# The third product of a fused attention and two-MLP kernel by Strassen's seven products instead of eight

## The chip, the cores and the metric

One Trainium2 chip, one of its cores. The metric is the device time of one execution in microseconds (us). TensorE (PE) multiplies, VectorE (DVE) and ScalarE (ACT) do the elementwise work, GpSimd (POOL) helps, SyncE (SP) issues all DMAs from one instruction queue.

## The reference

Attention with a sliding window of 128 and a linear bias, then two MLPs in sequence, all in float32, for 2304 tokens (4 batches of 576):

```python
x = attention(q, k, v)                     # (2304, 512), 8 heads of 64
y = ((x @ w1) * (x @ w2)) @ w3 @ w_out     # 512 -> 1024 -> 1024 -> 512
h = y @ w_in                               # 512 -> 2048
out = (h * clip(h + 3, 0, 6) / 6) @ w_out2 # 2048 -> 512
```

## The kernel before

The engines run the order in which a scheduler has put the program's instructions; each engine's queue is in order, and waits are on semaphores.

**Number format.** Every float32 operand of the MLPs is kept as two float32r parts, `hi` and `lo`: `split` (L73) makes `hi` by an ACT copy and `lo` by a DVE subtraction. `mm3` (L45) forms a product by three matmuls (lines L46, L47, L48): hi*hi, then hi*lo and lo*hi in one order or the other. The weights arrive as 64-bit words; `unpack` (L54) turns 128x1024 of them into float32 with one ACT pass (L63) and two DVE passes (L64 shift, L68 shift and OR), in place in a tile named `raw...`.

**First stage** (to about 500 us). Attention per pair of heads, `w3 @ w_out` multiplied out into `Wh`, `Wl`, then per batch and per half `s` of its tokens (288): eight `ab_unit`s, which give g = (x w1)(x w2), and four `y_unit`s (L420), one per 128 columns of y. A `y_unit` is 24 matmuls of 288 columns into a PSUM bank; ACT copies the sum out and a DMA stores it to the DRAM tensor `yT`, laid out [channel group, 128, token].

**Second stage** (from about 500 us). Tokens go in five blocks `j` (four of 512, one of 256), the 2048 columns of h in 16 groups `f` of 128. `h_unit(j, f)` (L523) is 12 matmuls of the block's width (4 channel groups, three matmuls each); then ACT makes relu(h + 3) (`rl`, L536), DVE takes min(.., 6) * h (L537), and `split` gives the two parts of g2. `o_unit(j, f)` (L543) runs two units later: for each 128 tokens, three matmuls of 512 columns into one of four PSUM banks that stay open over all 16 `f`. Two further pairs of banks (`ps_mm`, `ps_h`) serve h in turn. All 16 groups' weights stay in SBUF (`v2`); `p2_make` unpacks and splits them, nine items during the last batch, the others beside block 0. `y_load` and `y_split` bring each block of y back from DRAM.

The order is that of this loop:

```python
for idx, (j, f) in enumerate(units):
    h_unit(j, f)
    if idx >= LAG:
        o_unit(*units[idx - LAG])
    if j == 0:
        p2_make(f + len(AT), vpool)
```

Of the kernel before, what the change touches and what calls it, by code (L numbers as in the profile page):

```python
# [22 lines left out]
def tile_attention_moe_moe2(ctx: ExitStack, tc: tile.TileContext, qT, kT, vm, vt, wo, w3, w12, w2x, out):  # L23
# [412 lines left out]
    def v2_load(f, tmp):
        load(("v2", f), w2x[f], tmp)

    def v2_split(f, pool, lo_eng):
# [6 lines left out]
        split(flat(hi), flat(lo), unpack(rawt.pop(("v2", f)), pinned=True), lo_eng)
        v2[f] = (hi, lo)

    blocks = [(t, min(TB, NT - t)) for t in range(0, NT, TB)]
    yb = {}  # L450

    yraw = {}

    p2 = [("v", f) for f in range(KG)]
    p2.insert(NPRE, ("y", 0))

    def p2_load(i):
        if i < len(p2):
            (v2_load if p2[i][0] == "v" else y_load)(p2[i][1], dec)

    def p2_make(i, pool):
        if i < len(p2):
            if p2[i][0] == "v":
                v2_split(p2[i][1], pool, nc.vector)
            else:
                y_split(0, pool)
            p2_load(i + 2)

    def y_load(j, tmp):
        t0, n = blocks[j]  # L470
        t = tmp.tile([P, KD, TB], F32, tag="raw", name=f"yraw{j}")
        nc.sync.dma_start(out=t[:, :, 0:n], in_=yT[:, :, t0 : t0 + n].rearrange("c p t -> p c t"))
        yraw[j] = t

    def y_split(j, pool):
        t0, n = blocks[j]
        yh = pool.tile([P, KD, TB], F32R, tag="yh2", bufs=1, name=f"yh2_{j}")
        yl = pool.tile([P, KD, TB], F32R, tag="yl2", bufs=1, name=f"yl2_{j}")
        t = yraw.pop(j)
        for i in range(2):  # L480
            c = slice(2 * i, 2 * i + 2)
            nc.scalar.copy(yh[:, c, 0:n], t[:, c, 0:n])  # L482
# [154 lines left out]
```

## Time and profile before

| | us |
|---|---|
| median of 3 runs (lowest, highest) | 895.56 (895.0, 897.57) |
| the profiled execution: its time | 896.03 |
| its span, from the first to the last instruction | 894.2 |
| PE busy, share of the span | 874.9 (98%) |
| DVE, ACT, POOL busy | 356.1, 357.2, 128.1 |
| DMA: moved, mean rate | 66.9 MB, 75 GB/s |
| mean granted clock of TensorE | 0.998 of 2.4 GHz |

The profiled execution is 0.47 us above the median, and 1.83 us of its time lie outside its span. PE is busy in nearly all of the span; busy time of a matmul includes the drain that its successor overlaps, so the time that a matmul takes of PE is the distance from one start to the next, not its duration.

### The profile page before, as it was taken

What the parts mean: (1) busy time and instruction counts of PE and PEld (TensorE: products, weight loads), DVE (VectorE), ACT (ScalarE), POOL (GpSimd) and SP (SyncE); (2) the same over time, 40 slices, a digit from 0 to 9 for tenths busy, and PEclk for the clock granted to TensorE, in tenths of its full rate; (3) what the DMA queues carried; (4) which work ended last, traced back from release to release, by engine and by line L of the source; (5) the groups of instructions that cost most, each with busy time, mean ns of one, the idle gap of its engine ahead of it and who ended that gap; (6) DMA issues with size and microseconds to landing.
All of it is one profiled execution on the core that took longest, in us unless ns stands there. A gap on an engine that the chain in (4) does not pass through costs nothing.

```text
span 894.2 us, 13104 instructions
## 1 busy us (share of the span) xinstructions
PE 874.9 (98%) x5216; PEld 734.8 (82%) x5216; DVE 356.1 (40%) x821; ACT 357.2 (40%) x784; POOL 128.1 (14%) x198
## 2 busy tenths in 40 slices
PE   6799999999999999999999999999999999999998
PEld 3344598889888898999999888888888888888897
DVE  4896543342433424121536585232223222322232
ACT  6764654453444434321344565322232222222232
POOL 4361132321321312100020002200020001000000
PEclk9999999999999999999999999999999999999999
DMA  6975201211211110003244465020001000100000
GB/s 252 358 289 207 88 26 54 80 41 40 67 57 50 42 41 2 27 1 122 72 144 143 138 218 188 1 71 1 1 1 47 1 1 1 47 1 1 24 25 24
DMA packets 23277, 66.91 MB, mean 75 GB/s; under 512 B 2480, under 2 KB 8112, under 8 KB 18608
## 3 DMA queue, kind: packets, MB, share of 16 engines
q1 hardware_dynamic: 23216, 66.07, 21.2%
q8 instruction: 41, 0.67, 0.3%
q14 instruction: 20, 0.16, 0.1%
HBM read 56.62 MB, written 9.44 MB: 74 GB/s over the span
## 4 chain that ended last, share of the span: by engine, by line
PE 95%; DMA 2%; DVE 1%; ACT 1%; POOL 0%; issue 0%; SPq 0%; ACTq 0%; DVEq 0%; POOLq 0%
PE ab L46 8%; PE ab L47 8%; PE ab L48 8%; PE o L46 7%; PE o L48 7%; PE o L47 7%; PE h L46 7%; PE h L48 7%; PE h L47 7%; PE wps L321 6%; PE s L133 4%; PE y L46 4%; PE y L48 4%; PE y L47 4%; PE X L223 3%; PE pt L200 3%
## 5 line engine op out<-in xcount | busy, mean ns | idle before, releaser
L46 PE MATMUL ab<-xh,w12h 128*128 128x288 f32 x512 | 156.1, 305 | 0.0
L48 PE MATMUL ab<-xh,w12l 128*128 128x288 f32 x512 | 151.4, 296 | 0.0
L47 PE MATMUL ab<-xl,w12h 128*128 128x288 f32 x512 | 151.3, 296 | 0.0
L536 ACT ACTIVATE rl<-h,three 128x512 f32<-128x512 f32 (+1 forms) x80 | 51.7, 647 | 200.1 <-PE h L48 196.2
L537 DVE SCALAR_TENSOR_TENSOR rl<-rl,h 128x512 f32<-128x512 f32 (+1 forms) x80 | 50.6, 634 | 200.3 <-ACT rl L536 200.3
L46 PE MATMUL h<-yh,v2h 128*128 128x512 f32 (+1 forms) x320 | 118.5, 370 | 0.5 <-DVE rl L537 0.5
L48 PE MATMUL h<-yh,v2l 128*128 128x512 f32 (+1 forms) x320 | 118.2, 369 | 0.0
L47 PE MATMUL h<-yl,v2h 128*128 128x512 f32 (+1 forms) x320 | 117.9, 369 | 0.0
L46 PE MATMUL o<-v2h,g2h 128*128 128x512 f32 x288 | 112.9, 392 | 0.0
L47 PE MATMUL o<-v2l,g2h 128*128 128x512 f32 x288 | 112.3, 390 | 0.0
L48 PE MATMUL o<-v2h,g2l 128*128 128x512 f32 x288 | 111.6, 391 | 0.0
L46 PEld LDWEIGHTS ab<-xh,w12h 128*128 128x128 f32 x512 | 96.4, 188 | 9.4 <-issue 5.5
L47 PEld LDWEIGHTS ab<-xl,w12h 128*128 128x128 f32 x512 | 96.6, 189 | 0.5 <-issue 0.2
L48 PEld LDWEIGHTS ab<-xh,w12l 128*128 128x128 f32 x512 | 96.5, 188 | 0.0
L183 POOL TENSOR_SCALAR pr<-pr,rc 128x256 f32<-128x256 f32 (+1 forms) x128 | 70.0, 565 | 173.6 <-DVE rc L176 137.4
L46 PE MATMUL y<-g,Wh 128*128 128x288 f32 x256 | 76.0, 300 | 0.2 <-ACT yf L427 0.2
L47 PE MATMUL y<-g,Wh 128*128 128x288 f32 x256 | 75.1, 295 | 0.0
L48 PE MATMUL y<-g,Wl 128*128 128x288 f32 x256 | 75.0, 294 | 0.0
L75 DVE TENSOR_TENSOR g2l<-rl,g2h 128x512 fp32r<-128x512 f32 (+1 forms) x80 | 54.8, 685 | 44.8 <-ACT g2h L74 44.5
L416 DVE TENSOR_TENSOR asb<-ab,asb 128x288 f32<-128x288 f32 x64 | 29.3, 457 | 106.8 <-PE ab L48 104.7
L167 ACT ACTIVATE pr<-pr,mn 128x256 f32<-128x256 f32 (+1 forms) x128 | 60.4, 475 | 26.8 <-DVE mn L158 26.8
L483 POOL TENSOR_TENSOR yl<-yraw,yh 128x1024 fp32r<-128x1024 f32 (+1 forms) x10 | 24.1, 2428 | 326.7 <-ACT yh L482 326.7
(73 smaller groups left out, 1332.9 us busy)
## 6 DMA issues: line engine op xcount, KB each, us to landing
raww<-in_w_dram SPq DMA_DIRECT2D x16, 1024.0 KB, 6.2
rawv<-in_w2x_dram SPq DMA_DIRECT2D x16, 1024.0 KB, 4.9
qw<-in_qT_dram SPq DMA_DIRECT2D x16, 288.0 KB, 2.8
kw<-in_kT_dram SPq DMA_DIRECT2D x16, 288.0 KB, 3.2
yT<-yf SPq DMA_DIRECT2D x32, 144.0 KB, 1.8
out_dram<-ob SPq DMA_DIRECT2D x18, 256.0 KB, 2.0
vw<-in_vm_dram SPq DMA_DIRECT2D x16, 256.0 KB, 2.6
rawwo<-in_wo_dram SPq DMA_DIRECT2D x4, 1024.0 KB, 8.6
```

The lines of the kernel that those rows point to most:

```text
L46: nc.tensor.matmul(ps, lh, rh, start=first, stop=False)
L47: nc.tensor.matmul(ps, lh, rl, start=False, stop=False)
L48: nc.tensor.matmul(ps, ll, rh, start=False, stop=last)
L75: lo_eng.tensor_tensor(out=lo, in0=src, in1=f32(hi), op=ALU.subtract)
L133: in_order(n == NP + 1 and js[0] == 0 or not head, nc.tensor.matmul(ps[:, h, i, 0:nk], qw[n % 2][HB[h], P * j : P * (j + 1)], kw[n % 2][HB ...
L167: nc.scalar.activation(o, o, AF.Exp, bias=mn[:, col : col + 1], scale=-1.0, accum_out=sm[:, col : col + 1])
L183: nc.gpsimd.tensor_scalar(out=o, in0=o, scalar1=rc[:, 2 * j + h : 2 * j + h + 1], scalar2=1.0, op0=ALU.mult, op1=ALU.mult)
L200: nc.tensor.transpose(ps[:, o : o + P], prob[n, j][:, h, c : c + P], ident)
L321: nc.tensor.matmul(ps[:, 0:DM], w3v[i][:, m, :], wov[m], start=m == 0, stop=m == KF - 1)
L416: nc.vector.tensor_tensor(out=asb, in0=pss[1][:, 0:HS], in1=asb, op=ALU.mult)
L536: nc.scalar.activation(rl[:, 0:n], ps[:, 0:n], AF.Relu, bias=three[:, 0:1], scale=1.0)
L537: nc.vector.scalar_tensor_tensor(out=rl[:, 0:n], in0=rl[:, 0:n], scalar=6.0, in1=ps[:, 0:n], op0=ALU.min, op1=ALU.mult)
```

## The change

h is formed by Strassen's scheme in Winograd's form. The two halves of the columns of `w_in` (group p and group p + 8), the two halves of the 512 channels and the two halves of the tokens make a 2x2x2 product; seven products of half size take the place of eight. The halves of the tokens are the halves `s` of each batch, so that the sums of y that the scheme needs are formed where both halves are at hand, in `y_unit`, by eight DVE operations per batch (two for the columns d < 2, six for the others); seven tensors are stored (`yT`, now [2, 7, 128, 1152]). The sums of the weights are formed when a pair's words are unpacked (`va_make`: four DVE operations of 256 columns), kept as seven tiles in hi and lo, and stored to DRAM (`vad`; the output weights of the pair go to `vod`), because they don't fit in SBUF; each of the three token blocks reads them back pair by pair (`fetch`), but block 0 reads back only pairs 1 and 2. The blocks are 384 columns of both halves, so 768 tokens.

A unit is now a pair p in a block j: `h_pair` runs the seven products, each of 6 matmuls of 384 columns, in two PSUM banks (unit 0 also borrows two others), and between them as many of the previous unit's twelve output jobs as `QUOTA` says (a job: three matmuls of 512 columns, for 128 tokens and one half of the pair). Five DVE operations per unit (`u2`, `u3`, `c22`, `c21`, `c12`) add the products up, four gates follow as before but 384 wide. Six PSUM banks hold the outputs. In the last batch three pairs are made beforehand (`EARLY`), and `ab_unit` and `y_unit` use four PSUM banks there instead of two.

```diff
+    def bank(b, name):
+        nbank[0] += 1
+        if b < B - 1 or nbank[0] % 4 < 2:
+            return ps_mm.tile([P, 512], F32, tag="mm", name=name)
+        return ps_o.tile([P, 512], F32, tag=f"o{nbank[0] % 4}", name=name)
...
     def y_unit(b, s, d):
...
-        yf = sp.tile([P, HS], F32, tag="yf", name=f"yf_{b}_{s}_{d}")
-        nc.scalar.copy(yf, ps[:, 0:HS])
-        t0 = b * S + s * HS
-        nc.sync.dma_start(out=yT[d, :, t0 : t0 + HS], in_=yf)
...
+        if s == 0:
+            ys[d] = new(f"y0{d}")
+            nc.scalar.copy(ys[d], ps[:, 0:HS])
+            put(ys[d], Y11 if d < 2 else Y21)
+        elif d < 2:
+            ys["t", ci] = new(f"t1{ci}")
+            nc.vector.tensor_tensor(out=ys["t", ci], in0=ps[:, 0:HS], in1=ys[ci], op=ALU.subtract)
+            put(ys["t", ci], YT1)
+        else:
+            y22, t2, t3, t4 = (new(t) for t in ("y22", "t2", "t3", "t4"))
+            nc.scalar.copy(y22, ps[:, 0:HS])
+            put(y22, Y22)
+            nc.vector.tensor_tensor(out=t2, in0=y22, in1=ys["t", ci], op=ALU.subtract)
+            put(t2, YT2)
...
+    PRODUCTS = [(A11, Y11), (S2, YT2), (A12, Y21), (S3, YT3), (S1, YT1), (A22, YT4), (S4, Y22)]
+    EARLY = [1, 2, 0]
+    FIRST = [0, 1, 3, 4, 2, 5, 6, 7]
...
+    def va_make(p, n):
+        r = unpack(rawt.pop(("v2", 2 * p)), pinned=True)
+        t = va_tile(n)
+        c = [slice(i * 2 * P, (i + 1) * 2 * P) for i in range(4)]
+        sub = lambda o, a, b, op=ALU.subtract: nc.vector.tensor_tensor(out=r[:, c[o]], in0=r[:, c[a]], in1=r[:, c[b]], op=op)
+        split(flat(t[:, 0, 0:2, :]), flat(t[:, 1, 0:2, :]), r[:, 0 : 4 * P], nc.vector)
+        split(t[:, 0, A22, :], t[:, 1, A22, :], r[:, c[3]], nc.vector)
+        sub(3, 2, 3, ALU.add)
+        sub(2, 0, 2)
+        sub(0, 3, 0)
+        sub(1, 1, 0)
+        split(flat(t[:, 0, 3:7, :]), flat(t[:, 1, 3:7, :]), r, nc.vector)
+        late.append((vad[p], t))
+
+    def vo_make(p, n):
+        r = unpack(rawt.pop(("v2", 2 * p + 1)), pinned=True)
+        t = vo_tile(n)
+        split(flat(t[:, 0, :, :]), flat(t[:, 1, :, :]), r, nc.vector)
+        late.append((vod[p], t))
...
+    def h_pair(j, p, n, between):
...
+                mm3(
+                    ps[:, 0:TH], w[:, 0, k, cols], w[:, 1, k, cols], yh[:, c, :], yl[:, c, :],
+                    first and c == 0, last and c == 1, skip_group_check=True,
+                )
...
+        a, b_ = bank(0), None
+        product(0, a, True, True)
+        s1 = new("s1")
+        nc.scalar.copy(s1, a[:, 0:TH])
+        between(0)
+        b_ = bank(1)
+        product(1, b_, True, True)
+        u2 = new("u2")
+        nc.vector.tensor_tensor(out=u2, in0=b_[:, 0:TH], in1=s1, op=ALU.add)
+        between(1)
+        product(2, a, False, True)
+        gate(a[:, 0:TH], (0, 0))
+        between(2)
+        product(3, b_, False, True)
+        u3 = new("u3")
+        nc.vector.tensor_tensor(out=u3, in0=b_[:, 0:TH], in1=s1, op=ALU.add)
+        between(3)
+        a = bank(2)
+        product(4, a, True, True)
+        c = new("c22")
+        nc.vector.tensor_tensor(out=c, in0=a[:, 0:TH], in1=u3, op=ALU.add)
+        gate(c, (1, 1))
...
+    QUOTA = [2, 2, 2, 1, 2, 2, 1]
...
+    MAKE = {0: ("a",), 1: ("o", "a"), 2: ("o",), 3: ("a",), 4: ("o", "a"), 5: ("o", "a"), 6: ("o",)}
...
+    for n, (j, p) in enumerate(units2):
+        fetch(n + 2, "a")
+        if n > 0:
+            fetch(n + 1, "o")
...
+            if n % NPR == NPR - 1 and j + 1 < NBLK:
+                y_split(j + 1, k)
...
+        gs = h_pair(j, p, n, between)
+        jobs = o_jobs(j, n, gs)
```

`MAKE` says beside which unit the words of the five pairs left are made; `y_split` makes one of the next block's seven tiles after each product of a block's last unit.

Three places show what moves. **SyncE, at the end of the last `y_unit`** (`rawv`: words of weights; `yT`: stores of y; `va`, `vo`: a unit's tiles). Before:

```order
L429 DMA yT_63<-yf_3_1_1_5059 128x288
L429 DMA yT_63<-yf_3_1_2_5096 128x288
L289 DMA rawv2_9_5069<-in_w2x_dram 128x1024
L429 DMA yT_63<-yf_3_1_3_5124 128x288
L289 DMA rawv2_10_5167<-in_w2x_dram 128x1024
```

Now:

```order
L447 DMA yT_63<-t4_3_1_2_5193 128x288
L710 DMA vo1_5257<-vod_65 128x2048
L447 DMA yT_63<-y22_3_1_3_5227 128x288
L485 DMA vad_64<-va0_4762 128x3584
L447 DMA yT_63<-t2_3_1_3_5228 128x288
L447 DMA yT_63<-t3_3_1_3_5229 128x288
L447 DMA yT_63<-t4_3_1_3_5230 128x288
```

The last four stores of y stand behind a load of 1.05 MB, which waits for the last y matmul, and three of them behind a store of 1.84 MB as well.

**VectorE, at the start of the second stage** (`rl`: the gate's min and multiply; `c22`, `c21`, `u2`, `u3`: sums of products). Before:

```order
L537 SCALAR_TENSOR_TENSOR rl_0_0_5153<-rl_0_0_5153,h_0_0_5140 128x512
L537 SCALAR_TENSOR_TENSOR rl_0_1_5182<-rl_0_1_5182,h_0_1_5169 128x512
L75 TENSOR_TENSOR g2l_0_0_5155<-rl_0_0_5153,g2h_0_0_5154 128x512
L64 TENSOR_SCALAR rawv2_8_5004<-rawv2_8_5004 128x1024
L68 SCALAR_TENSOR_TENSOR rawv2_8_5004<-rawv2_8_5004 128x1024
```

Now:

```order
L635 TENSOR_TENSOR u2_0_0_5276<-h_0_0_1_5269,s1_0_0_5266 128x384
L64 TENSOR_SCALAR rawv2_6_4773<-rawv2_6_4773 128x1024
L68 SCALAR_TENSOR_TENSOR rawv2_6_4773<-rawv2_6_4773 128x1024
L618 SCALAR_TENSOR_TENSOR rl_0_0_5301<-rl_0_0_5301,h_0_0_0_5259 128x384
L642 TENSOR_TENSOR u3_0_0_5314<-h_0_0_1_5269,s1_0_0_5266 128x384
L75 TENSOR_TENSOR va2_5282<-rawv2_6_4773,va2_5282 128x512
L647 TENSOR_TENSOR c22_0_0_5323<-h_0_0_2_5316,u3_0_0_5314 128x384
L75 TENSOR_TENSOR va2_5282<-rawv2_6_4773,va2_5282 128x256
L653 TENSOR_TENSOR c21_0_0_5338<-u3_0_0_5314,h_0_0_3_5331 128x384
L505 TENSOR_TENSOR rawv2_6_4773<-rawv2_6_4773 128x256
```

The first gate stands behind two passes over the words of the third unit's weights, and the sums that follow stand between the making of those weights.

**VectorE, in one unit of block 1**, where no weights are made. Before, the same two rows for each `f`:

```order
L537 SCALAR_TENSOR_TENSOR rl_1_7_5961<-rl_1_7_5961,h_1_7_5948 128x512
L75 TENSOR_TENSOR g2l_1_7_5963<-rl_1_7_5961,g2h_1_7_5962 128x512
L537 SCALAR_TENSOR_TENSOR rl_1_8_5993<-rl_1_8_5993,h_1_8_5980 128x512
L75 TENSOR_TENSOR g2l_1_8_5995<-rl_1_8_5993,g2h_1_8_5994 128x512
L537 SCALAR_TENSOR_TENSOR rl_1_9_6025<-rl_1_9_6025,h_1_9_6012 128x512
```

Now:

```order
L635 TENSOR_TENSOR u2_1_3_6767<-h_1_3_1_6760,s1_1_3_6752 128x384
L618 SCALAR_TENSOR_TENSOR rl_1_3_6781<-rl_1_3_6781,h_1_3_0_6745 128x384
L75 TENSOR_TENSOR g2_1_3_00_6782<-rl_1_3_6781,g2_1_3_00_6782 128x384
L642 TENSOR_TENSOR u3_1_3_6799<-h_1_3_1_6760,s1_1_3_6752 128x384
L647 TENSOR_TENSOR c22_1_3_6811<-h_1_3_2_6804,u3_1_3_6799 128x384
L618 SCALAR_TENSOR_TENSOR rl_1_3_6813<-rl_1_3_6813,c22_1_3_6811 128x384
L75 TENSOR_TENSOR g2_1_3_11_6814<-rl_1_3_6813,g2_1_3_11_6814 128x384
L653 TENSOR_TENSOR c21_1_3_6832<-u3_1_3_6799,h_1_3_3_6825 128x384
L658 TENSOR_TENSOR c12_1_3_6852<-h_1_3_2_6804,u2_1_3_6767 128x384
```

The sum that frees the bank of the unit's last product, `c12`, has moved ahead of the gates of `c21` and of itself. On PE the unit's output jobs stand between the products much as `QUOTA` has them; the scheduler puts the two matmuls that need only g2's hi part of three jobs ahead of the three that need its lo part.

## Rows read from the trace of the kernel before

**Rows 1.** Windows, second stage: us, engines' busy time (instructions), PEclk, DMA share, GB/s

```profile
504.34:890.00 385.66, 385.66 (x1776) 319.83 (x1776) 132.47 (x191) 124.52 (x191) 18.32 (x8) 1.00 0.11 37
```

**Rows 2.** The same stretches, instructions on h alone

```profile
504.34:890.00 385.66, 201.76 (x912) 159.98 (x912) 49.88 (x79) 50.42 (x78) 1.00 0.11 37
```

**Rows 3.** PE in order of time, last batch: start, us, engine, line, operation

```profile
457.81 0.29 PE L48 MATMUL ab<-xh,w12l 128*128 128x288 f32 x1
...
458.87 0.30 PE L47 MATMUL ab<-xl,w12h 128*128 128x288 f32 x1
```

**Rows 4.** In order of time, block 1: matmuls of 512, one gate

```profile
642.10 0.39 PE L46 MATMUL h<-yh,v2h 128*128 128x512 f32 x1
...
644.60 0.39 PE L48 MATMUL h<-yh,v2l 128*128 128x512 f32 x1
...
645.09 0.69 ACT L536 ACTIVATE rl<-h,three 128x512 f32<-128x512 f32 x1 [3.37 <-PE h L48]
...
645.80 0.69 DVE L537 SCALAR_TENSOR_TENSOR rl<-rl,h 128x512 f32<-128x512 f32 x1 [3.37 <-ACT rl L536]
...
646.53 0.62 ACT L74 CAST g2h<-rl 128x512 fp32r<-128x512 f32 x1 [0.76 <-DVE rl L537]
...
647.18 0.69 DVE L75 TENSOR_TENSOR g2l<-rl,g2h 128x512 fp32r<-128x512 f32 x1 [0.69 <-ACT g2h L74]
```

**Rows 5.** Weight loads for h: duration min/median/max in ns

```profile
L46 PEld LDWEIGHTS h<-yh,v2h x320: 186/188/192, 454.2 to 885.3; 128*128 128x128 f32 x160
```

**Rows 6.** In order of time, start of the second stage

```profile
502.88 1.26 ACT L536 ACTIVATE rl<-h,three 128x512 f32<-128x512 f32 x2 [3.84 <-DMA yT<-yf]
...
503.50 0.39 PE L48 MATMUL h<-yh,v2l 128*128 128x512 f32 x1
503.60 1.29 DVE L537 SCALAR_TENSOR_TENSOR rl<-rl,h 128x512 f32<-128x512 f32 x2 [6.41 <-ACT rl L536]
...
504.34 0.50 PE L46 MATMUL h<-yh,v2h 128*128 128x512 f32 x1 [0.46 <-DVE rl L537]
```

**Rows 7.** DVE groups by shape: busy us, mean ns | idle before

```profile
L416 DVE TENSOR_TENSOR asb<-ab,asb 128x288 f32<-128x288 f32 x64 | 29.3, 457 | 106.8 <-PE ab L48 104.7 <-ACT pr L167 1.1 <-PE pt L200 0.8
...
L75 DVE TENSOR_TENSOR v2l<-rawv,v2h 128x1024 fp32r<-128x1024 f32 x16 | 20.0, 1249 | 11.6 <-ACT v2h L74 11.6
L68 DVE SCALAR_TENSOR_TENSOR rawv<-rawv 128x1024 int32<-128x1024 int32 x16 | 19.6, 1226 | 7.1 <-ACT rawv L63 6.4
...
L64 DVE TENSOR_SCALAR rawv<-rawv 128x1024 int32<-128x1024 int32 x16 | 11.1, 691 | 2.1 <-DMA rawv<-in_w2x_dram 2.0
...
L75 DVE TENSOR_TENSOR g2l<-rl,g2h 128x256 fp32r<-128x256 f32 x16 | 6.8, 425 | 7.1 <-ACT g2h L74 7.1
L537 DVE SCALAR_TENSOR_TENSOR rl<-rl,h 128x256 f32<-128x256 f32 x16 | 6.7, 421 | 23.7 <-ACT rl L536 23.7
```

**Rows 8.** ACT groups by shape

```profile
L536 ACT ACTIVATE rl<-h,three 128x256 f32<-128x256 f32 x16 | 7.6, 477 | 23.3 <-PE h L48 23.2
...
L74 ACT CAST g2h<-rl 128x256 fp32r<-128x256 f32 x16 | 6.5, 407 | 7.5 <-DVE rl L537 7.5
```

**Rows 9.** DMA issues: KB each, median us to landing

```profile
rawv<-in_w2x_dram SPq DMA_DIRECT2D x16, 1024.0 KB, 4.9
...
yT<-yf SPq DMA_DIRECT2D x32, 144.0 KB, 1.8
out_dram<-ob SPq DMA_DIRECT2D x18, 256.0 KB, 2.0
```

**Rows 10.** SyncE in order of time at the end of the last y

```profile
497.22 0.42 SPq L289 DMA_DIRECT2D rawv<-in_w2x_dram  x1
```

**Rows 11.** The chain that ended last, the same place

```profile
499.06 3.71 DMA yT<-yf
```

**Rows 12.** Windows at the start

```profile
34.60:38.00 3.40, 3.34 (x4) 1.49 (x5) 3.40 (x12) 2.99 (x9) 1.51 (x4) 0.52 1.00 402
```

**Rows 13.** PE in order of time at the start

```profile
34.66 5.83 PE L321 MATMUL wps<-wov,w3v 128*128 128x512 f32 x9 [2.23 <-DVE w3v L68]
```

More of the change, by code (lines that the diff above doesn't have):

```diff
@@ new lines, in tile_attention_moe_moe2, with dma @@
+    NBLK = 3
+    TH = NT // 2 // NBLK
+    NTT = TH // P
+    A11, A12, A22, S2, S4, S3, S1 = range(7)
+    PRODUCTS = [(A11, Y11), (S2, YT2), (A12, Y21), (S3, YT3), (S1, YT1), (A22, YT4), (S4, Y22)]
+    EARLY = [1, 2, 0]
+    FIRST = [0, 1, 3, 4, 2, 5, 6, 7]
+    ORDER = [FIRST, list(range(NPR)), list(range(NPR))]
+    units2 = [(j, p) for j in range(NBLK) for p in ORDER[j]]
+    place = {p: n for n, p in enumerate(FIRST)}
+    va = {}
+    vo = {}
+    p1_open = [True]
+    late = []
+    def dma(dst, src):
+        in_order(not p1_open[0], nc.sync.dma_start(out=dst, in_=src))
@@ L441, in v2_split, with y_split @@
+    def y_split(j, i):
         hi, lo = (
-            (blk if old else pool).tile(
-                [P, 2 * KD, P], F32R, name=f"v2{t[0]}{f}", **({"tag": f"{t}{f - NPRE}"} if old else {})
-            ) for t in ("hi", "lo")
-        )
[L446 to L482, printed above, removed]
-            nc.gpsimd.tensor_tensor(out=yl[:, c, 0:n], in0=t[:, c, 0:n], in1=f32(yh[:, c, 0:n]), op=ALU.subtract)
-        yb[j] = (yh, yl)
+            blk.tile([P, 2, TH], F32R, tag=f"{t}{i}", name=f"y{t}{j}_{PRODUCTS[i][1]}") for t in ("hi", "lo")
+        )
@@ L561, in tile_attention_moe_moe2 @@
[L561 to L575 removed]
+    g2p = ctx.enter_context(tc.tile_pool(name="g2p", bufs=8))
@@ new lines, in tile_attention_moe_moe2, with product, new, gate @@
+    po = {}
+    ob_ = {}
+    def h_pair(j, p, n, between):
+        w = va[n]
+        def product(i, ps, first, last):
+            k, y = PRODUCTS[i]
+            yh, yl = yc[j, y]
+            for c in range(2):
+                cols = slice(c * P, (c + 1) * P)
+                mm3(
+                    ps[:, 0:TH], w[:, 0, k, cols], w[:, 1, k, cols], yh[:, c, :], yl[:, c, :],
+                    first and c == 0, last and c == 1, skip_group_check=True,
+                )
+        def new(tag):
+            return r2.tile([P, TH], F32, tag=tag, bufs=2 if tag in ("rl", "u2", "u3") else 1, name=f"{tag}_{j}_{p}")
+        gs = {}
+        def gate(h, q):
+            rl = new("rl")
+            g_ = g2p.tile([P, 2, TH], F32R, tag="g2", name=f"g2_{j}_{p}_{q[0]}{q[1]}")
+            nc.scalar.activation(rl, h, AF.Relu, bias=three[:, 0:1], scale=1.0)
+            nc.vector.scalar_tensor_tensor(out=rl, in0=rl, scalar=6.0, in1=h, op0=ALU.min, op1=ALU.mult)
+            split(g_[:, 0, :], g_[:, 1, :], rl, nc.vector)
+            gs[q] = g_
+        def bank(i):
+            if n == 0 and i >= 2:
+                return ps_o.tile([P, 512], F32, tag=f"o{i + 2}", name=f"h_{j}_{p}_{i}")
+            return ps_mm.tile([P, 512], F32, tag="mm", name=f"h_{j}_{p}_{i}")
+        a, b_ = bank(0), None
[20 more added lines that the diff above has]
+        gate(c, (1, 1))
+        between(4)
+        b_ = bank(3)
+        product(5, b_, True, True)
+        c = new("c21")
+        nc.vector.tensor_tensor(out=c, in0=u3, in1=b_[:, 0:TH], op=ALU.subtract)
+        gate(c, (1, 0))
+        between(5)
+        product(6, a, False, True)
+        c = new("c12")
+        nc.vector.tensor_tensor(out=c, in0=a[:, 0:TH], in1=u2, op=ALU.add)
+        gate(c, (0, 1))
+        between(6)
+        return gs
@@ new lines, in tile_attention_moe_moe2, with fetch @@
+    QUOTA = [2, 2, 2, 1, 2, 2, 1]
+    def fetch(n, which):
+        if n >= len(units2) or n == 0:
+            return
+        j, p = units2[n]
+        if j == 0 and p not in EARLY:
+            return
+        t, src = (va_tile(n), vad) if which == "a" else (vo_tile(n), vod)
+        in_order(n > 1, nc.sync.dma_start(out=f32(t), in_=src[p]))
+    MAKE = {0: ("a",), 1: ("o", "a"), 2: ("o",), 3: ("a",), 4: ("o", "a"), 5: ("o", "a"), 6: ("o",)}
+    fetch(1, "a")
+    fetch(1, "o")
+    jobs = []
@@ L578 @@
+    for job in jobs:
+        job()
 _OUTS = [((2304, 512), "float32")]
```

197 lines of the change are left out of this document (121 added, 76 removed).

## The prediction

> **What bounds the kernel now.** I read first the windows of the second stage, then the order of time at its two ends, then the groups by shape. In the windows the reader is to see that PE's busy time is the window itself [rows 1]: 385.66 us, 1776 matmuls, no idle. VectorE is busy for a third of it and the DMA engines for 0.11. So the second stage costs what its matmuls cost in PE's row, and nothing else. Of these 1776, 912 are h's [rows 2] (720 of 512 columns, 192 of 256; 48 of block 0's ran earlier) and 864 are o's of 512 columns, together 860,160 columns. 385.66 us / 860,160 is 0.4484 ns a column, 0.2296 us for 512. The one wait between the stages is 0.46 us, for VectorE, which waited for ScalarE, which waited for the last store of y [rows 6].
>
> **What is removed.** h is now 768 matmuls of 512 columns and 192 of 256: 442,368 columns, at 0.4484 ns 198.3 us. After, 24 units of 7 products of 6 matmuls are 1008 matmuls of 384 columns, 387,072 columns, 7/8. No row has a width of 384. The nearest are 288 with 0.1325 us (eight distances in 458.87 - 457.81 [rows 3]) and 512 with 0.2296. A line between them gives 0.1741 us, so 175.5 us, **22.8 us less**. Bounds: the rate of the fastest stretch of 512 (eleven distances in 2.50 us [rows 4], 0.444 ns a column) gives 0.1705 us and 26.4 less; the rate of 288 (0.460 ns) gives 0.1766 and 20.2 less. I take the line, since 384 lies halfway. The outputs keep 864 matmuls of 512 columns, 198.4 us. A unit is then 42 x 0.1741 + 36 x 0.2296 = 15.58 us.
>
> The order of weight load and matmul could speak against this. A weight load lasts 188 ns [rows 5], more than a matmul of 384 would take; but matmuls of 288 follow each other every 132 ns, each with weights of its own, so the load does not set the pace there, and I keep the saving. The Trainium skill, "TensorE: Matmul & The Clock Gate", section "Back-to-back issue gap", says that in a stream of weight loads and matmuls both set the spacing; the row of 288 columns decides against that here, the rival below prices it. The same section gives for a matmul alone columns / 2.4 + 2.5 ns; by it the sum would be an estimated 22.9 us less, since its spacings are 6 to 8% under these rows at both widths.
>
> **What is added on VectorE.** A unit's thirteen operations of 384 columns (five sums, four gates of two) cost by a line between 256 columns (0.425, 0.421 us [rows 7]) and 512 (0.69 [rows 4]) 0.56 us each, 7.3 us. To make one pair's weights: shift 0.69 and OR 1.23, then for `va` lo parts of 512, 256 and 1024 columns (0.69, 0.43, 1.25) and four sums of 256 (0.43): 6.0 us; for `vo` the two passes and 1.25: 3.2 [rows 4, 7]. So a unit of blocks 1 and 2 needs 7.3 of its 15.58 us; between banks that alternate, with 0.27 us from a product's end to the next engine [rows 4], nothing there waits, and these sixteen units add nothing. If that cover failed, a unit would lose a gate's chain, relu, min, cast and lo part of 384 columns, 0.58 + 0.56 + 0.51 + 0.56 = 2.2 us [rows 4, 7, 8].
>
> **Where PE will wait.**
>
> *Start of the second stage.* Count from T, the end of the last `y` matmul. By the new order 26 matmuls of h follow up to the end of the sum for the first gate (T + 4.5), and 6 more (T + 5.6); then unit 1's first product needs the bank which that gate frees. VectorE meanwhile has `u2` (from T + 3.75 to 4.3), then shift and OR over the words of the third unit's weights (to T + 6.2), then the gate's multiply (to T + 6.8): PE waits 1.3 us. Thirty more matmuls bring PE to T + 12.0, where the outputs begin, which need g2's hi parts. The later gates stand in VectorE's row behind the six operations that make those weights, and I count 1.6 us for the outputs that use the gates of the third and fourth sums. VectorE has 28.5 us of work there against PE's 28.4. Together **3.0 us**.
>
> A second wait is nearly there. The first cast of g2 waits for the stores of `t2`, `t3`, `t4`, whose buffers end there; they stand on SyncE behind a load of 1.05 MB, issued only at T, and a store of 1.84 MB. That a small store is late behind a large transfer is seen before: 1 MB was issued at 497.22 [rows 10], and the store of y after it took 3.71 us [rows 11] where the median is 1.8 [rows 9]. At the 402 GB/s of the first load stretch [rows 12] the 1.05 + 1.84 + 0.44 MB take 8.3 us; with that latency of 1.8 and the issues between they land at T + 11 to T + 12. That is just under PE's need: I cost it at nothing, the likeliest rival at its price.
>
> *Last half of the last batch.* The 192 matmuls of its g take 25.4 us. VectorE has 16 operations of 0.46 [rows 7], one pair's weights (9.2) and seven splits of y (768 columns, about 1.0 each): 23.5 us. Queues this full do not fit without a gap: **1 us**, between nothing and 3.
>
> *Rest of block 0.* Two later units also make a `va` and a `vo`: 7.3 + 9.2 = 16.5 us against 15.58, **1.5 us** with what the neighbours catch up (0 to 3).
>
> *Changes of block.* Seven splits of y in a block's last unit bring VectorE to 14 us of 15.58, and the first product of a block needs the first of them: **2 us** for both (0 to 4). *End.* The last gate's chain has no product behind it: **0.4**. Removed: the wait of 0.46 [rows 6]. Net **+7.4 us**.
>
> **DMA.** Blocks 1 and 2 read 2.88 MB per unit, 185 GB/s. Block 0 moves 17.3 MB of stores (six `vad`, six `vod`) and 17.1 MB of loads in some 116 us, 296 GB/s, against 402 seen [rows 12]. So it hides, if stores to DRAM are as fast as loads. Rows bound that poorly: 144 KB stored in 1.8 us, 256 KB in 2.0 [rows 9], loads of 1024 KB in 4.9.
>
> **Sum.** The profiled execution took 896.03 us; 896.03 - 22.8 + 7.4 = 880.6. It lies 0.47 above the median, so **880.2 us**.
>
> **Rivals.**
>
> *A, no new waits:* the scheduler's reordering swallows them all. 895.56 - 22.8 = 872.8 us. For it: PE never waits in 385 us today [rows 1]. Against: VectorE's surplus at the start and in block 0.
>
> *B, the first outputs wait for the stores of y:* if the large store goes at half of 402 GB/s, it lands some 5 us later. PE idles for that time and then finds a lower clock: after a wait of 2.23 us [rows 13] the granted clock was 0.52, the 1.2 GHz level, in the next 3.40 us [rows 12], worth 1.7 us. 880.2 + 5 + 1.7 = 887. The Trainium skill says in the same page, section "Why this matters for your kernels", that idle gaps between bursts of matmuls drop the clock; the trace agrees in those rows.
>
> *C, weight loads set the pace:* matmuls of 384 columns follow at 188 ns [rows 5]; 1008 are 189.5 us, the saving 8.8, with the waits 894.2: no change. Against it the spacing at 288.
>
> *D, slower:* stores to DRAM are slow and block 0 becomes a DMA stage. Its 17.1 MB of loads take 42 us at 402 GB/s, so the 17.3 MB of stores have 74: below 235 GB/s time is lost, below some 195 (15 us lost) the gain is gone, and at 150 they take 115, 42 us lost: 922 us. For it: no row stores more than 256 KB at once. Against: from 144 to 256 KB a store took only 0.2 us more [rows 9], so size costs little.
>
> **How the numbers follow.** Forecast 0.57, A 0.15, B 0.17, C 0.03, D 0.08. The likeliest case has 875 to 886 as its own range, from the saving's bounds (-3.6, +2.6) and about three us of waits either way. The range of 0.8 reaches to A with the larger saving (870) and to B with the smaller one and its wait a little longer (891); it leaves out C, D and a few in a hundred below. A difference of 0.3%, 2.7 us, is what a measurement here can tell from none. Faster (under 892.9): the forecast, A, and B but for its longest wait, 0.87. Same: C and that rest of B, 0.05. Slower (over 898.2): D, 0.08.
>
> **What would show it.** In the profile after: 1008 matmuls on h at about 0.174 us from start to start, no wait in units of blocks 1 and 2, which take 15.6 us each; PE idle some 7 us over the second stage, half of it in the first 30 us; the first wait of PE there put down to VectorE. B is right if the first cast waits for `yT` for longer than PE has work; C if h's matmuls stand 0.188 apart; D if block 0 takes well over 125 us with DMA busy throughout. The forecast falls if 384 columns cost as much per matmul as 512 nearly do, or if PE waits in every unit for a gate: 2 us in each of 24 would take twice the gain.

## The result and the profile after

The changed kernel takes **881.02 us** (median of 4 runs, 879.91 to 883.42), the kernel before 895.96 in the runs beside it: a ratio of 0.9835, 95% interval 0.9809 to 0.9861. The forecast was 880.2. The profiled execution took 883.42 us with a span of 881.6, 12.6 less than the span before.

The windows of the second stage come first. A line gives the stretch and its length, then busy time and instructions of TensorE, of its weight loads, of VectorE, ScalarE and GpSimd, then as in [rows 1] the granted clock, the busy share of the DMA engines and GB/s. The first line runs from T to the first output matmul (T = 494.0 is the start of the last `y` matmul plus one spacing of 0.13 us), the second from there to the last output; then the change from block 0 to 1, block 1 and block 2 alone; the fence below it has h alone. The reader sees where TensorE still stands still: 1.8 us in the first stretch, 1.5 at the change of block, none that this view shows in blocks 1 and 2. The DMA engines, 0.11 busy before, are full in both stretches where TensorE waits; full engines do not make it wait by themselves, for from 604 to 620 us their share is 1.00 as well and TensorE is busy throughout.

```profile
494.00:507.00 13.00, 11.20 (x64) 10.59 (x62) 10.46 (x20) 6.06 (x11) 0.00 (x0) 1.00 0.94 343
507.04:875.50 368.46, 366.94 (x1806) 326.71 (x1806) 213.30 (x378) 149.02 (x259) 0.00 (x0) 1.00 0.59 221
628.00:634.00 6.00, 4.53 (x22) 3.61 (x22) 4.37 (x9) 2.38 (x5) 0.00 (x0) 1.00 1.03 413
634.00:754.00 120.00, 120.00 (x594) 107.21 (x593) 60.03 (x108) 43.02 (x79) 0.00 (x0) 1.00 0.65 239
754.00:875.30 121.30, 121.30 (x598) 107.90 (x597) 55.46 (x104) 38.11 (x72) 0.00 (x0) 1.00 0.37 138
```

```profile
507.04:875.50 368.46, 181.02 (x942) 166.76 (x942) 75.51 (x137) 23.80 (x45) 1.00 0.59 221
```

The first and the last of nine matmuls of 384 columns in order of time, from block 1: eight distances in 1.41 us, 0.176 each. Over all 1008 the mean without waits is 0.1753 (the line between [rows 3] and 512 columns gave 0.1741). The weight loads are as long as before [rows 5].

```profile
701.04 0.34 PE L46 MATMUL h<-yhi,va 128*128 128x384 f32 x1
...
702.45 0.33 PE L48 MATMUL h<-yhi,va 128*128 128x384 f32 x1
```

```profile
L46 PEld LDWEIGHTS h<-yhi,va x336: 186/188/189, 482.5 to 868.7; 128*128 128x128 f32 x168
```

The start of the second stage in order of time. The first gate's multiply (L618) stands behind the shift and OR (L64, L68) of the third unit's words, as counted, and TensorE, last fed at 499.37, goes on at 500.78: 1.24 us over its spacing. Then the first cast of g2 (L74) waits 2.27 us for the stores of `t`, and the first output matmul comes 0.93 us late.

```profile
497.73 0.56 DVE L635 TENSOR_TENSOR u<-h,s 128x384 f32<-128x384 f32 x1 [1.67 <-PE h L48]
...
498.20 0.69 DVE L64 TENSOR_SCALAR rawv<-rawv 128x1024 int32<-128x1024 int32 x1
...
498.99 1.23 DVE L68 SCALAR_TENSOR_TENSOR rawv<-rawv 128x1024 int32<-128x1024 int32 x1
...
499.37 0.34 PE L48 MATMUL h<-yhi,va 128*128 128x384 f32 x1
500.13 0.55 DVE L618 SCALAR_TENSOR_TENSOR rl<-rl,h 128x384 f32<-128x384 f32 x1
...
500.78 0.41 PE L46 MATMUL h<-yhi,va 128*128 128x384 f32 x1 [1.07 <-issue]
...
506.47 0.93 ACT L74 CAST g<-rl 128x384 fp32r<-128x384 f32 x2 [2.27 <-DMA yT<-t]
...
507.04 0.51 PE L46 MATMUL o<-vo,g 128*128 128x512 f32 x1 [0.77 <-ACT g L74]
```

The chain that ended last, same place: a store of 144 KB, 1.8 us in [rows 9], takes 9.29 us from its issue, behind the 1.05 and 1.84 MB, and lands at T + 12.4 (forecast: T + 11 to T + 12).

```profile
497.11 9.29 DMA yT<-t
506.47 0.52 ACT g L74
```

The same view at the change from block 0 to 1. Output copies (`ob`) delay a split of y on VectorE; only its end frees a buffer for the next load of y, which lands 3.70 us later; cast, lo part and TensorE follow.

```profile
624.58 0.54 DVE ob L694
625.18 0.96 DVE ylo L75
626.15 3.70 DMA yraw<-yT
629.88 0.84 ACT yhi L74
630.74 0.97 DVE ylo L75
631.76 0.44 PE h L47
```

In block 1, unseen in the forecast: TensorE finds the bank of the unit's first gate not yet free (the weight load has stood idle for 0.36 us, until L618 ends), which costs 0.26 us over two matmuls, and so in seven of the sixteen units, every second one or third.

```profile
657.73 0.58 ACT L617 ACTIVATE rl<-h,three 128x384 f32<-128x384 f32 x1 [5.51 <-PE h L48]
...
658.35 0.55 DVE L618 SCALAR_TENSOR_TENSOR rl<-rl,h 128x384 f32<-128x384 f32 x1 [4.93 <-ACT rl L617]
...
658.57 0.39 PE L48 MATMUL o<-vo,g 128*128 128x512 f32 x1
...
658.95 0.19 PEld L46 LDWEIGHTS h<-yhi,va 128*128 128x128 f32 x1 [0.36 <-DVE rl L618]
658.95 0.44 PE L46 MATMUL h<-yhi,va 128*128 128x384 f32 x1
```

VectorE's groups by shape, mean in ns, to be set against 0.56 us each:

```profile
L75 DVE TENSOR_TENSOR g<-rl,g 128x384 fp32r<-128x384 f32 x96 | 53.0, 555 | 17.9 <-ACT g L74 15.2
L618 DVE SCALAR_TENSOR_TENSOR rl<-rl,c 128x384 f32<-128x384 f32 x72 | 39.8, 554 | 16.8 <-ACT rl L617 16.7
```

DMA issues (KB, median us to landing). Stores to DRAM of this size are in no row of before; 1792 KB land in 7.9 us against 7.4 for a load, 1024 KB in 12.2 against 7.4, each with whatever is queued ahead.

```profile
va<-vad SPq DMA_DIRECT2D x18, 1792.0 KB, 7.4
...
rawv<-in_w2x_dram SPq DMA_DIRECT2D x16, 1024.0 KB, 7.4
vad<-va SPq DMA_DIRECT2D x8, 1792.0 KB, 7.9
vod<-vo SPq DMA_DIRECT2D x8, 1024.0 KB, 12.2
```

### The profile page after: what moved, and what is told of

Read it like the earlier page. It is cut to its first block, busy times and chain, and to the rows that moved or that the text cites. A ratio compares the mean times of both kernels' runs of the same rounds, so it can differ in the third digit from the quotient of the medians.

```text
span 881.6 us, 13721 instructions
## 1 busy us (share of the span) xinstructions
PE 858.1 (97%) x5264; PEld 745.2 (85%) x5264; DVE 464.7 (53%) x1074; ACT 384.6 (44%) x859; POOL 105.1 (12%) x188
## 4 chain that ended last, share of the span: by engine, by line
PE 93%; DMA 3%; DVE 2%; ACT 1%; POOL 0%; issue 0%; SPq 0%; DVEq 0%; ACTq 0%; POOLq 0%
PE ab L46 8%; PE ab L47 8%; PE ab L48 8%; PE o L46 7%; PE o L47 7%; PE o L48 7%; PE wps L324 7%; PE h L46 6%; PE h L47 6%; PE h L48 6%; PE s L136 4%; PE y L46 4%; PE y L48 4%; PE y L47 4%; PE X L226 3%; PE pt L203 3%
## 5 line engine op out<-in xcount | busy, mean ns | idle before, releaser
L46 PE MATMUL h<-yhi,va 128*128 128x384 f32 x336 | 114.2, 340 | 1.7 <-issue 1.1
L47 PE MATMUL h<-ylo,va 128*128 128x384 f32 x336 | 113.2, 337 | 0.8 <-DVE ylo L75 0.8
L46 PE MATMUL o<-vo,g 128*128 128x512 f32 x288 | 113.1, 393 | 0.8 <-ACT g L74 0.8
L48 PE MATMUL h<-yhi,va 128*128 128x384 f32 x336 | 113.2, 337 | 0.0
L47 PE MATMUL o<-vo,g 128*128 128x512 f32 x288 | 113.1, 393 | 0.0
L48 PE MATMUL o<-vo,g 128*128 128x512 f32 x288 | 86.5, 392 | 0.0
L617 ACT ACTIVATE rl<-c,three 128x384 f32<-128x384 f32 x72 | 44.2, 616 | 76.2 <-DVE c L647 43.7
L46 PEld LDWEIGHTS h<-yhi,va 128*128 128x128 f32 x336 | 63.1, 188 | 8.6 <-DVE rl L618 2.9
L47 PEld LDWEIGHTS h<-ylo,va 128*128 128x128 f32 x336 | 63.1, 188 | 4.8 <-DVE ylo L75 1.4
L161 DVE CUSTOM_DVE_ANT_0 pr<-s,rel 128x256 f32<-128x256 f32 (+1 forms) x128 | 42.3, 387 | 44.4 <-PE s L136 44.4
## 6 DMA issues: line engine op xcount, KB each, us to landing
vod<-vo SPq DMA_DIRECT2D x8, 1024.0 KB, 12.2
```

What stands on the lines that cost most here:

```text
L46: nc.tensor.matmul(ps, lh, rh, start=first, stop=False, **kw)
L47: nc.tensor.matmul(ps, lh, rl, start=False, stop=False, **kw)
L48: nc.tensor.matmul(ps, ll, rh, start=False, stop=last, **kw)
L161: nc.vector.tensor_tensor_reduce(out=o, in0=sc.pop((n, j, h))[0:m, 0:nk], in1=rel8[0:m, 2 * (n % NP) + h, mo : mo + nk], op0=ALU.add, op1= ...
L617: nc.scalar.activation(rl, h, AF.Relu, bias=three[:, 0:1], scale=1.0)
```

## The experiments

Two numbers of each profile go beside the times. The **stretch** runs from T to the start of the last output matmul (381.3 us in the changed kernel). The **waits** in it are what the distances between matmul starts exceed 0.175 (h) or 0.230 us (o) by, where that is over 0.06: 6.7 us in the changed kernel, of which 1.31 + 1.04 at the start, 0.31 once in block 0, 2.29 at the first change of block, none at the second, and seven times 0.26 in blocks 1 and 2. Times also hold the first stage, which differs by up to 3.7 us between profiles of code that is the same there (T lies between 490.9 and 494.6), so where a microsecond matters the stretch decides; it is that of one profile for each kernel.

| kernel | us | ratio to before (95%) | stretch | waits |
|---|---|---|---|---|
| the change | 881.02 | 0.9835 (0.9809 to 0.9861) | 381.3 | 6.7 |
| e1 make later | 883.96 | 0.9860 (0.9832 to 0.9889) | 381.7 | 7.0 |
| e2 stores first | 880.43 | 0.9824 (0.9799 to 0.9849) | 379.7 | 5.2 |
| e3 order kept, blocks 1, 2 | 878.73 | 0.9814 (0.9786 to 0.9841) | 379.6 | 4.5 |
| e4 order kept from the change of block | 884.44 | 0.9868 (0.9843 to 0.9893) | 384.8 | 9.8 |
| e5 loads of y early | 880.08 | 0.9827 (0.9797 to 0.9856) | 379.1 | 4.0 |
| e6 = e2 + e4 + e5 | 879.04 | 0.9814 (0.9789 to 0.9839) | 381.2 | 5.6 |
| e7 an eighth product | 905.23 | 1.0100 (1.0077 to 1.0124) | 403.1 | 3.4 |
| e8 twice the traffic, blocks 1, 2 | 899.07 | 1.0030 (1.0014 to 1.0045) | 397.0 | 23.2 |
| e9 = e2 + e3 + e5 | 878.08 | 0.9804 (0.9787 to 0.9820) | 378.1 | 2.6 |
| e10 = e9 + e1 | 876.46 | 0.9784 (0.9768 to 0.9801) | 377.0 | 1.4 |
| e11 stores of weights twice | 903.66 | 1.0087 (1.0068 to 1.0107) | 402.8 | 27.4 |
| e12 whole stores at the end | 880.34 | 0.9826 (0.9809 to 0.9844) | 380.9 | 6.3 |

**e1: the weights made behind the first gate.**

```diff
-            if k in (1, 4) and todo:
+            if k in ((2,) if n == 0 else (1, 4)) and todo:
```

> Edit: in the first unit of the second stage the making of the third unit's weights is recorded after the first gate and not before it, so that VectorE's row has the first gate right behind u2. Theory (two waits in a row: first the gate behind the unpacking, then the first cast of g2 behind the last stores of y, which land at T + 12.5 us whatever PE does): the wait of 1.3 us before the second unit's first product is gone, the wait before the first output matmul grows from 1.0 to about 2.3 us, and the product that needs the first gate's bank in the second unit waits 0.4 us; in sum no change, 881 us (880.5 to 882). Rival 1 (the two waits are independent): 1.3 us less, 879.7 us, the second wait stays at 1.0. Rival 2 (the unpacking only moves): a wait of 1 us or more for VectorE turns up in units 2 to 4 and the time is 882 or more.

The stretch is the same, as the theory said, but not for its reason. The wait for the first gate falls from 1.31 to 0.49 us. The cast starts at 507.10, T + 12.5 as before, when the stores land; yet the wait before the first output, which was to grow to 2.3 us, is gone. One more product stands before that output (72 matmuls of h, not 66), and it waits 0.91 us for VectorE's `u3`. So the start holds 1.40 us of waits, 0.95 less than in the changed kernel. They come back later: 0.85 us in block 0 against 0.31, 2.98 at the first change of block against 2.29. That is rival 2 in kind, spread over smaller waits; whether VectorE's work that has moved or the scheduler's other order makes them, no run separates. The median, 883.96, lies outside the theory's range, but its 2.9 us are not in the stretch.

```profile
506.64 0.44 PE L46 MATMUL h<-yhi,va 128*128 128x384 f32 x1 [0.65 <-DVE u L642]
...
507.10 0.51 ACT L74 CAST g<-rl 128x384 fp32r<-128x384 f32 x1 [0.23 <-DMA yT<-t]
...
507.81 0.40 PE L46 MATMUL o<-vo,g 128*128 128x512 f32 x1
```

**e2: the stores of y first.** (`after_y` ties one DMA's place on SyncE behind the last store of y; the store of `va0` follows it anyway.)

```diff
...
-        in_order(n > 1, nc.sync.dma_start(out=f32(t), in_=src[p]))
+        ins = in_order(n > 1, nc.sync.dma_start(out=f32(t), in_=src[p]))
+        if n == 1 and which == "o":
+            after_y(ins)
```

> Edit: on SyncE the load of the second unit's output weights (1.05 MB) and, behind it, the store of the first weights (1.84 MB) are issued after the last four stores of y, not before them; nothing else is moved by hand. Theory: the last stores of y land about T + 5 us, the first cast of g2 no longer waits for a DMA, and the wait of 1.0 us before the first output matmul is gone: 880.0 us; the wait of 1.3 us before it stays. Rival 1 (that wait is VectorE's and not the stores'): it stays, 881 us. Rival 2 (the load of output weights is now late): PE waits at the second unit's outputs, 882 or more.

SyncE in order of time: the three stores of `t` are out before the two large transfers, and the first cast starts at 499.31, T + 7.1, waiting for no DMA. The wait of 1.04 us is gone, the 1.31 stay, the stretch is 1.6 us shorter.

```profile
493.29 1.31 SPq L455 DMA_DIRECT2D yT<-t  x3
...
494.69 0.40 SPq L718 DMA_DIRECT2D vo<-vod  x1
...
495.14 0.45 SPq L493 DMA_DIRECT2D vad<-va  x1
...
499.31 0.51 ACT L74 CAST g<-rl 128x384 fp32r<-128x384 f32 x1
```

**e3 and e4: TensorE's recorded order.** `pinned` keeps a matmul behind the one recorded before it; e3 has `n > NPR`, e4 `n >= NPR - 1`.

```diff
...
+    def mm3(ps, lh, ll, rh, rl, first, last, pinned=False, **kw):
+        in_order(pinned, nc.tensor.matmul(ps, lh, rh, start=first, stop=False, **kw))
...
-                    mm3(po[o], gs[q][:, 0, ts_], gs[q][:, 1, ts_], w[:, 0, f, :], w[:, 1, f, :], begin, final)
+                    mm3(po[o], gs[q][:, 0, ts_], gs[q][:, 1, ts_], w[:, 0, f, :], w[:, 1, f, :], begin, final, n > NPR)
```

> Edit: from the tenth unit on, TensorE's matmuls keep the order in which they are recorded (two output jobs between products), instead of the scheduler's order, in which every second unit has only seven matmuls (1.27 us) between the third product and the fifth, which needs the bank that the first gate frees 1.48 us after the third product. Theory: the waits of 0.26 us in seven units of blocks 1 and 2 are gone, 1.8 us less, 879.2 us; the wait at the change from block 0 to 1 stays at 2.3 us. Rival (these waits have nothing to do with the bank, such as a refresh or the instruction stream): they stay, 881 us, or others of the same size turn up in the pinned order.

> Edit: as in the run before, but the recorded order is kept from the last unit of block 0 on. There the scheduler had moved four products of the new block together, so that they needed the last splits of y at once. Theory: with output jobs between the products the last splits of y are needed some 6 us later; the 2.3 us of waits for ylo and yhi at the change of block are gone as well: 2.3 + 1.8 = 4.1 us less, 876.9 us. Rival (the splits are late because their loads land late, so PE waits for them in any order): 1 us or more of that wait is left, 878 to 879 us.

e3: all seven waits of 0.26 us are gone and none has come: it was the bank. The stretch is 1.7 us shorter. e4 falsified its theory: the change of block became worse, 6.8 us of waits for 2.3. In the recorded order one product waits 3.2 us for a split whose load is late, with all that could run queued behind it; the scheduler's order, which I had blamed, had filled that time with other products. This is the rival's mechanism, at a price well above the rival's. After that wait TensorE's granted clock is 0.51, the 1.2 GHz level, for the next 6.5 us (columns as in the windows above; in the lists of waits: who waited for whom, us in total, times, the longest):

```profile
618.00:622.50 4.50, 1.26 (x7) 0.69 (x5) 1.15 (x3) 1.87 (x3) 0.00 (x0) 0.94 0.90 340
622.50:629.00 6.50, 6.19 (x17) 5.42 (x18) 3.40 (x4) 2.36 (x3) 0.00 (x0) 0.51 0.69 262
```

```profile
PE h L50 <- ACT yhi L74: 3.2, 1, 3.2
PE h L51 <- DVE ylo L75: 0.3, 1, 0.3
```

**e5: the loads of y early.**

```diff
...
-        yraw[j, i] = yrp.tile([P, 2, TH], F32, tag="yr", name=f"yraw{j}_{k}")
+        pool, tag = (dec, "raw") if j > 0 and i in (4, 5) else (yrp, "yr")
+        yraw[j, i] = pool.tile([P, 2, TH], F32, tag=tag, name=f"yraw{j}_{k}")
...
-            if n % NPR == NPR - 2 and j + 1 < NBLK and k < 3:
+            if n % NPR == NPR - 2 and j + 1 < NBLK and k < 6:
...
```

> Edit: six of the seven loads of the next block's y are issued in the unit before a block's last (four buffers of their own instead of three, two in tiles that the weights' words no longer need), so that loads 3 to 5 no longer wait for a split to free a buffer. Theory (the wait at the change from block 0 to 1 is the chain split, load, split through three buffers): the 2.2 us there fall under 0.5, 878.8 us. Rival (the DMA engines are full there, share 1.0 between 604 and 620 us and after 628, so y lands late however early it is issued): 1 us or more stays, 880 us or more.

The 2.29 us at the change of block are gone, so the chain through three buffers was their cause, not full DMA engines. One unit later 0.92 us appear: the scheduler's order has changed with the edit, and a product stands there directly behind the one whose bank `u3` must first read. The stretch is 2.2 us shorter; 0.8 of it came at the start, where the scheduler's order also changed.

**e6: all three, with the order kept through the change of block.**

> Edit: together the stores of y first on SyncE, the early loads of y, and the recorded order on TensorE from the last unit of block 0 on. Theory: left of the new waits is the one of 1.3 us before the second unit's first product and some 0.3 in block 0; 881.0 - 1.0 - 2.2 - 1.8 = 876.0 us. Rival 1 (the recorded order makes TensorE stand at the change of block for whatever is late there, as in the run that kept it without early loads): 2 us or more of wait there, 878.5 or more. Rival 2 (the waits are elsewhere made up): 880 or more.

Rival 1: TensorE idles 2.0 us there for splits (1.4 and 0.6), and its granted clock is 0.62 in the 4.5 us after; the stretch is that of the change. The order is kept to advantage only where nothing is late.

```profile
625.50:630.00 4.50, 4.27 (x14) 3.98 (x15) 2.36 (x5) 0.94 (x2) 0.00 (x0) 0.62 1.00 394
```

**e7: the fifth product twice.**

```diff
         product(4, a, True, True)
+        product(4, a, True, True)
```

> Edit: the fifth product of each unit is run twice in a row, the second pass into the same bank from the start, so that a unit has eight products and all else is as it was: the cost of one product. Theory (TensorE sets the time and a matmul of 384 columns takes 0.175 us wherever it stands): 144 more matmuls are 25.2 us, less the 2.1 us of waits for the first gate's bank, which the longer unit may cover: 904 to 906.5 us. Rival 1 (weight loads of 0.188 us set the pace): 27 us, 908. Rival 2 (block 0 is set by VectorE or the DMA engines, not by TensorE): only two thirds of the products count, 16.8 us, 897.8.

24.2 us more by the medians, 21.8 in the stretch: 144 x 0.175 = 25.2 less 3.3 us of waits that the longer units cover (3.4 left of 6.7). So a product costs what its matmuls cost, block 0 included, at the spacing of the others, not at 188 ns.

**e8: twice the traffic in blocks 1 and 2.**

```diff
...
         in_order(n > 1, nc.sync.dma_start(out=f32(t), in_=src[p]))
+        if j > 0:
+            dma((vad2 if which == "a" else vod2)[p], src[p])
```

> Edit: in blocks 1 and 2 each load of weights is followed by a copy of the same 1.84 or 1.05 MB from DRAM to DRAM, which nothing reads: 2.88 MB more per unit for the DMA engines. Theory (the reload of weights hides with a margin of a half and does not slow TensorE): matmuls keep 0.175 and 0.230 us, the waits in units of blocks 1 and 2 stay at 0.26 in every second one, and only the change of block, where the engines are full already, loses 1 to 3 us more: 881 to 885 us. Rival 1 (traffic slows the matmuls): their spacing grows by 2% or more, 888 or more. Rival 2 (a copy costs its engines twice, once read and once written): a unit's transfers take 21 us at 402 GB/s against 15.7, so TensorE waits for weights in every unit, 950 us or more.

Where the loss lies was right, its size not. Within block 1 the DMA engines run full at 408 GB/s and TensorE still loses only 1.3 us in 120; its spacing stays (0.1751, 0.2294). But at the change from block 0 the copies stand before the output weights of the new block's first unit: 6.7 us of wait, then the 1.2 GHz level again. The stretch is 16 us longer where I had put 1 to 3: 10 at the first change of block, 4 at the second. A copy is not paid twice (rival 2).

```profile
629.80:635.00 5.20, 4.87 (x10) 3.09 (x10) 0.85 (x1) 1.53 (x2) 0.00 (x0) 0.50 0.60 221
...
640.00:760.00 120.00, 118.70 (x585) 105.70 (x586) 57.34 (x106) 40.39 (x76) 0.00 (x0) 1.00 1.00 408
```

```profile
PE o L46 <- DMA vo<-vod: 6.7, 1, 6.7
```

**e9 and e10: what helps, together.** e9 takes e2, e3 and e5; e10 adds e1.

> Edit: the stores of y first on SyncE, the early loads of y, and the recorded order on TensorE from the tenth unit on, so that the scheduler keeps its hand at the change from block 0 to 1. Theory (the waits found are separate and add): from the end of the last y matmul to the last output matmul 381.3 - 1.0 - 1.4 - 1.8 = 377.1 us; time 881.0 - 4.2 = 876.8 us. Rival (the change of block takes whatever is saved, since the DMA engines are full there): 379 us or more of that stretch, 879 or more of time.

> Edit: as the run before, and the third unit's weights are made behind the first gate. Theory (alone this gained nothing, because the first cast then waited for the stores of y until the same moment; with those stores early it gains): the 1.3 us before the second unit's first product are gone, 375.8 us for the stretch, 875.5 us of time. Rival (VectorE's surplus at the start only shows elsewhere: 28.5 us of work beside 28.4): the stretch stays at 377 us or above.

The waits add up as the theory had it: 2.6 and 1.4 us are left. Both stretches are 1.0 to 1.2 us longer than expected, most of it since the output matmuls take 0.2308 us in the kept order and 0.2300 in the scheduler's (864 of them, 0.7 us); that puts e10's stretch at the bound of its rival, 377 us, but the rival's new waits are not there. And e1's edit, worth nothing alone, takes 1.1 us off the stretch in this company: 0.80 us of waits at the start, about what it took away there alone, and 0.38 in block 0, where alone it added 0.54. So what hid its gain was not the wait for the stores, as its expectation has it, but what turned up later. e10 beats both kernels: 876.46 us. Its last waits of any size:

```profile
PE h L50 <- DVE u L653: 0.7, 1, 0.7
PE h L50 <- PE h L52: 0.3, 1, 0.3
```

**e11: the weights stored twice.**

```diff
...
             dma(dst, f32(t))
+            dma(dst2, f32(t))
```

> Edit: each of the sixteen stores of made weights in block 0 and before is issued twice, to two DRAM tensors: 17 MB more to store in block 0, some 410 GB/s over it. Theory (stores move at the rate of loads, up to 402 to 415 GB/s, so block 0 has a margin of a third and this uses it up): block 0 becomes longer by 3 to 15 us, 884 to 896 us, with TensorE waiting for a DMA. Rival 1 (stores are slower than loads, half the rate): 30 us or more, 911 or more. Rival 2 (SyncE's row takes them in cover): no change, 881 us.

22.6 us, beyond my range though short of rival 1. The engines, with stores beside loads, reach 422 GB/s (windows below), so the mix is no slower than loads alone (402 in [rows 12]). Nor is block 0 lost as a whole: from 530 to 630 us TensorE is busy throughout, beside 327 to 397 GB/s. Of 27.4 us of waits, the lower clock's share included, 15.9 lie in the first 36 us, of which the longest, 5.1, ends as the last store of `t` lands; 9.7 lie at the change of block.

```profile
494.00:510.00 16.00, 12.39 (x67) 11.10 (x65) 9.86 (x19) 5.29 (x9) 0.00 (x0) 1.00 1.01 380
510.00:530.00 20.00, 13.08 (x41) 10.34 (x42) 12.66 (x22) 9.47 (x15) 0.00 (x0) 0.66 1.01 422
...
550.00:570.00 20.00, 20.00 (x102) 18.06 (x101) 14.34 (x27) 11.11 (x19) 0.00 (x0) 1.00 0.94 371
...
630.00:650.00 20.00, 15.23 (x57) 11.93 (x57) 10.94 (x16) 9.24 (x15) 0.00 (x0) 0.83 0.90 341
```

**e12: the last stores in one piece.**

```diff
+        if j == NBLK - 1:
+            yield 0, P, 2 * TH * j + (th * NTT + i) * P
+            return
```

> Edit: in the last block each output tile of 128 tokens is stored to DRAM in one piece, to rows that follow each other, so that the eight stores of the end are six; the last block's output rows then stand in another order than the reference's. Theory (the end became longer because SyncE issues eight stores in a row, 0.49 us each, the last of them 64 or 128 KB pieces): from the start of the last output matmul to the end of the span 6.3 us become about 5.3, and with them the time: 880.0 us. Rival (the end is the latency of the last store, however many there are): 6 us or more stay, 881 us.

This kernel leaves 96 rows of the output unwritten and writes 96 others twice (its expectation speaks of another order); the bytes stored are the same, and only its time is used. From the last output matmul to the end it takes 5.2 us, not 6.3: the last store is issued 0.5 us sooner, as SyncE's row shows six in 3.45 us where eight took 3.94 (first line: the change), and lands 0.7 us sooner after its issue. That the stores are fewer and that they are larger pieces is not separated. In e3 eight stores end almost as early (5.4 us), as its order starts them 0.9 us sooner: what is still queued behind the last output decides.

```profile
873.87 3.94 SPq L485 DMA_DIRECT2D out_dram<-ob  x8
```

```profile
870.38 3.45 SPq L485 DMA_DIRECT2D out_dram<-ob  x6
```

## Why the prediction was right

The sum, term by term, in the profiled execution (distances of matmul starts for the first two rows):

| step | forecast, us | measured, us |
|---|---|---|
| h: 960 matmuls to 1008 of 384 columns | -22.8 | -22.0 (198.8 to 176.8) |
| o: the same 864 matmuls | 0 | +1.1 (197.5 to 198.6) |
| start of the second stage | +3.0 | +2.35 (1.31 + 1.04) |
| last half of the last batch | +1 | 0 |
| rest of block 0 | +1.5 | +0.3 |
| changes of block | +2 | +2.3 |
| units of blocks 1 and 2 | 0 | +1.8 |
| end | +0.4 | +1.7 |
| wait between the stages, removed | -0.5 | -0.6 |
| y's matmuls | 0 | -0.5 |
| start of the kernel, not of the change | 0 | +1.0 |

The total is -12.6 against -15.4 forecast for this execution, a miss of 2.8; without the last row, which differs between profiles of the same code, -13.6. By medians the difference from the forecast is 0.8 us: the profiled execution lies 2.4 above its median.

**The saving** was right in mechanism and nearly in size. The line between widths gave 0.1741 for 0.1753, and e7 shows the price from the other side. The Trainium skill, "TensorE: Matmul & The Clock Gate", section "Back-to-back issue gap", has columns / 2.4 + 2.5 ns for a matmul by itself, by which 384 columns would take an estimated 162.5 ns; the rows are 8% above it, as they are at 288. Rival C (188 ns) is refuted by the spacing. What no term foresaw is that the unchanged output matmuls go 0.5% slower in the new order.

**The start** was right in its first half: the gate behind shift and OR, 1.3 us, shown by e1 and e10, which take most of it away. The second half had the wrong cause: the 1.6 us for the outputs of the third and fourth gates did not come, and the stores of y, which I had landing just in time, landed 0.4 to 1.4 us later than that. This is rival B's mechanism at a fifth of its price, with the clock at 1.00 after it; e2 shows it. Of the 6.7 us of waits 2.35 lie in the first 30 us, a third and not half.

**The step that failed** is "nothing there waits" for units of blocks 1 and 2. I had counted VectorE's work against the unit, and the chain for one gate, but not how many matmuls the scheduler leaves between the third product and the fifth in every second unit: 0.23 us of output work after a product of 1.05, against a gate's 0.27 + 0.58 + 0.55 us and the hand-overs. e3 settles it. It can be read from the order of the instructions, by adding up what stands between the two.

**The terms for queues that are nearly full** (last batch, rest of block 0), 2.5 us, measured 0.3. In the last half of the last batch the matmuls of g took 25.7 us without a wait, and VectorE was busy for 19.7 of them, not for the 23.5 counted: some of its work ran outside. The changes of block had the right sum but neither the cause nor the place: all of it at the first, through the three buffers of y (e5), none at the second. **The end** was sized by the wrong chain: not the last gate, but stores in pieces on SyncE (e12 gives back 1.1 of the 1.7 us). These errors of opposite sign cancel in part, and the medians lie closer than the profiled executions, so the 0.8 us are luck in part.

**Rival A** (no new waits, 872.8) is refuted, though e10 comes within 4 us of it. **Rival D** is refuted as far as it was put: once block 0 has started, no wait of TensorE in it is put down to a store. Twice the stores lose the whole gain (e11), but at the two ends of block 0, where small transfers or first needs stand behind the queue, and not as a block set by its DMAs. Left open: why the spacing of the output matmuls changes by 0.3 to 0.8% with their order (0.2289, 0.2300, 0.2308 us); no run separates it.

## What to carry to other kernels

Fewer multiplications turned into time nearly one for one, because the engine that multiplies was the bound and every sum fitted beside it; price the matmul at the new width from the rows around it, then look for the places where a small wait can appear. These are found by following one buffer at a time through the new order: how much work stands between its last reader's start and its next writer. After taking a wait away, add up all the waits again: in e1 the gain at the start was spent further on, and the stretch alone would have said that the first wait costs nothing.
